# Three kinds of heads: scores and maxima from split q and k for heads 10 to 15, with p and v left whole

## The chip, the cores and the metric

The kernel runs on one core of one Trainium2 chip. A core has a matrix engine (TensorE, PE in the profile), a vector engine (VectorE, DVE), a scalar engine (ScalarE, ACT), a general engine (GpSimd, POOL) and a queue engine that issues transfers (SyncE, SP). Each takes its instructions in the order in which they stand in the program; they wait for one another through semaphores. Matrix products are written to PSUM, of which there are eight banks; everything else on the chip lies in SBUF. The metric is the device time of one execution in microseconds (us), the median of several runs.

## The reference

The first half is causal attention with a decay, over 8 batches of 8 heads, 576 positions and 64 channels (64 heads in all); the second half sends its output through two matrix products with a squared ReLU between them.

```
scores = q @ k.T / 8                     # per head, 576 x 576
cum    = cumsum(log(clip(f, 1e-4, 1)))
scores = where(causal, -1e9, scores + cum[:, None] - cum[None, :])
attn   = exp(scores - max(scores))
attn   = attn / (sum(attn) + 1e-9)
x      = (attn @ v), heads side by side  # 4608 x 512
out    = relu(x @ w_in)**2 @ w_out       # 512 -> 2048 -> 512
```

All is float32. A product of two float32 operands can be computed whole (one matmul on float32 data, which the trace records as two), or split: each operand is written as a rounded high part and a low remainder in the type float32r, and the result is the sum of a few float32r matmuls on these parts.

## The kernel before

**Slots.** The program is a list of slots, written out by a Python loop (L742 to L766). A slot is one *unit* of one head: a block of 128 keys against all the queries that may see it (for the first block, queries 256 to 575, and 0 to 255 as the sixth unit). Six units make a head, 64 heads make 384 slots. In a slot stand, in this order: the scores of the unit (`score`), the product of exponentials and v for the unit of two slots ago (`av_part`), a divide by the row sums that is due (`finish`), and then, in two halves, the events that are listed for this slot, some steps of the weight conversion (`cv`) and some of the second half of the network (`fill`). PE, ACT, DVE and POOL keep to this order; SP's transfers are put in order by the scheduler.

**Scores.** `score` puts scores transposed into a PSUM bank (keys on partitions, queries along the row). Decay and maximum ride along as rows of the operands beyond the 64 channels: k carries the cumulative sum, q carries the negative row maximum. ACT then takes the exponential straight into `p`. Units on the diagonal are masked.

**Two kinds of heads.** Heads 0 to 15 (`NWHOLE = 16`) are *whole*: q and k are loaded as float32 into `rl` (`load_whole`, SP), one float32 matmul makes the scores (L392), a small bf16 matmul adds the mask (L395), p stays float32, and one float32 matmul makes p times v (L456). Heads 16 to 63 are *split*: q and k are loaded once to `qkraw` (`load`, SP), and `prep` makes the parts: two casts on DVE into `rk` (L313, L314), two casts on ACT into `rl` (L315, L318), two subtractions on POOL into `rl` (L321, L324). Two float32r matmuls make the scores (L399, L402), POOL masks p (L411), p and v are split too (`split_p`: L424 on ACT, L425 on DVE; `split_v`: L332 on DVE, L333 on POOL), and p times v takes three float32r matmuls (L435 to L437).

**Maxima.** The row maxima of a head are found one head ahead by six float32r matmuls from `rk` (L346), each of which DVE reduces (L354). For a whole head `rk` is loaded by POOL with a cast during the transfer (`load_rounded`, L287), the six stand in slots 0 to 2.5 of the head before, and the maxima, which come out as a column, are turned into a row by five small matmuls (`turn_maxima`, L377) and two ACT copies (L381). For a split head `rk` comes from the casts, the six stand in slots 1.5 to 4, and each finished column is written to the row of `rk` by a transfer on SP (L359). The casts stand in slot 0.5, POOL's subtractions in slots 1.5 and 3.5.

**Banks.** `bank(use)` hands out PSUM banks in turn. From the first step of the second half on, maxima have no banks of their own and take turns with the scores: four banks at first, two (`s=[1, 2]`) from the first step of the second chunk of 256 tokens on, four again from the third.

**Second half.** `mlp1` (L555, twelve matmuls of 256 columns), ACT and DVE (L563 to L566), `mlp2` (L578, six of 512 columns). 18 chunks times 16 steps; `fill` spreads them over the slots from slot 53 on. Until about slot 95 a step can stand only where its weights are converted: the weights come as 64-bit patterns, and `weight_ops` makes float32 of them and splits it, for each of 32 tiles with ACT (L205, L210), four DVE instructions (L228, L233, L236, L240) and one POOL subtraction (L216).

The head whose scores are computed moves from 9 to 16 between about 97 and 224 us of the profiled execution. In this stage heads 9 to 15 compute scores while weights are still being converted and steps of the second half are already standing between them.

## Time and profile before

| | |
|---|---|
| three runs | 1218.88, 1219.85, 1225.44 us, median 1219.85 us |
| profiled execution | 1217.56 us, of which the span from the first to the last instruction is 1215.8 us |
| busy over the span | PE 1189.4 us (98%), DVE 769.5 (63%), ACT 706.2 (58%), POOL 361.8 (30%) |
| TensorE clock granted | 0.994 of full speed on average |
| PE in 0 to 95 us (start, heads 0 to 8) | busy 84.5 of 95 us |
| PE in 113.59 to 206.30 us (heads 10 to 14) | busy 89.8 of 92.7 us |
| PE in 410 to 800 us (split heads) | busy 389.2 of 390 us |

"Busy" is the time in which at least one instruction of the engine was running. Matmuls overlap in the records (one starts before the last one's results are out), so what a matmul costs in a full stream is not its own duration but the distance from its start to the start of the next one.

### The profile page before, as it was taken

To read this page: it belongs to the slowest core of one execution; us is meant where nothing else is said; L and a number is where in the kernel's file an instruction comes from. 1 tells how busy PE (TensorE), PEld (TensorE's weight loads), DVE (VectorE), ACT (ScalarE), POOL (GpSimd) and SP (SyncE) were. 2 spreads that over 40 slices of the span, in tenths; PEclk is the share of its full clock that TensorE was granted. 3 is DMA by queue.
4 is the path that set the end of the run, shared out by engine and by line. 5 is a ranking of instruction groups with operands and counts; after the bars stand their busy time and mean duration, and the time that the engine had idled before them with its cause. 6 is when DMAs were issued, how large, how long until landed. Compare 5 with 4: busy or idle time off the path is not lost.

```text
span 1215.8 us, 23255 instructions
## 1 busy us (share of the span) xinstructions
PE 1189.4 (98%) x7816; PEld 1047.3 (86%) x7816; DVE 769.5 (63%) x2031; ACT 706.2 (58%) x1736; POOL 361.8 (30%) x551
## 2 busy tenths in 40 slices
PE   6999999899999999999999999999999999999998
PEld 3668787779999898999999989988999899999997
DVE  5767776766767667665655766667676767533332
ACT  3875556566666666655556566666666666533232
POOL 3332322333334333322322333333333333200000
PEclk8999999999999999999999999999999999999999
DMA  7889310111211112111121212212121212000000
GB/s 217 206 198 272 90 42 26 47 46 42 59 42 53 38 47 50 41 49 27 43 55 21 53 32 44 57 42 58 37 50 33 58 43 58 12 28 11 9 18 18
DMA packets 104767, 72.16 MB, mean 59 GB/s; under 512 B 86573, under 2 KB 86573, under 8 KB 104649
## 3 DMA queue, kind: packets, MB, share of 16 engines
q1 hardware_dynamic: 103368, 65.96, 21.2%
q0 software_dynamic: 1280, 4.72, 1.6%
q8 instruction: 62, 1.02, 0.4%
q14 instruction: 57, 0.46, 0.1%
HBM read 60.51 MB, written 9.87 MB: 58 GB/s over the span
## 4 chain that ended last, share of the span: by engine, by line
PE 90%; ACT 4%; DVE 2%; issue 2%; DMA 1%; POOL 0%; SPq 0%; DVEq 0%; POOLq 0%; ACTq 0%
PE bank L555 33%; PE bank L578 31%; PE bank L346 4%; PE bank L392 3%; PE bank L435 3%; PE bank L456 3%; PE bank L402 3%; PE bank L437 3%; PE bank L436 3%; PE bank L399 3%; ACT r L563 1%; DVE bank L354 1%; ACT gh L565 0%; ACT den L471 0%; ACT p L409 0%
## 5 line engine op out<-in xcount | busy, mean ns | idle before, releaser
L578 PE MATMUL bank<-w,gh 128*128 128x512 f32 x1152 | 414.1, 400 | 0.0
L555 PE MATMUL bank<-xh,w 128*128 128x256 f32 x2304 | 329.0, 285 | 1.9 <-POOL w L216 1.9
L555 PEld LDWEIGHTS bank<-xh,w 128*128 128x128 f32 x2304 | 300.3, 189 | 10.3 <-POOL w L216 2.4
L425 DVE TENSOR_TENSOR pl<-p,ph 128x320 fp32r<-128x320 f32 (+4 forms) x288 | 177.4, 616 | 192.8 <-ACT ph L424 188.3
L578 PEld LDWEIGHTS bank<-w,gh 128*128 128x128 f32 x1152 | 217.5, 189 | 38.4
L563 ACT ACTIVATE r<-bank 128x256 f32<-128x256 f32 x288 | 110.6, 384 | 218.4 <-PE bank L555 172.3
L578 PE MATMUL bank<-w,gl 128*128 128x512 f32 x576 | 226.9, 394 | 0.2 <-DVE gl L566 0.2
L564 DVE TENSOR_TENSOR g<-r 128x256 f32<-128x256 f32 x288 | 125.7, 437 | 146.6 <-ACT r L563 146.0
L424 ACT CAST ph<-p 128x320 fp32r<-128x320 f32 (+4 forms) x288 | 119.4, 415 | 145.6 <-POOL p L411 103.0
L411 POOL TENSOR_SCALAR_AFFINE_SELECT p<-p 128x128 f32<-128x128 f32 (+1 forms) x240 | 77.1, 321 | 412.0 <-ACT p L409 317.6
L555 PE MATMUL bank<-xl,w 128*128 128x256 f32 x1152 | 184.5, 282 | 0.0
L555 PEld LDWEIGHTS bank<-xl,w 128*128 128x128 f32 x1152 | 158.2, 191 | 0.2 <-DVE xl L543 0.2
L566 DVE TENSOR_TENSOR gl<-g,gh 128x256 fp32r<-128x256 f32 x288 | 130.3, 452 | 36.2 <-ACT p L409 2.0
L354 DVE CUSTOM_DVE_ANT_0 bank<-bank,mz 128x256 f32<-128x256 f32 (+4 forms) x320 | 133.4, 433 | 22.6 <-PE bank L346 20.5
L409 ACT ACTIVATE p<-bank 128x320 f32<-128x320 f32 (+4 forms) x288 | 111.6, 388 | 60.1 <-PE bank L402 48.9
L565 ACT ACTIVATE gh<-r 128x256 fp32r<-128x256 f32 x288 | 120.6, 419 | 9.4
L346 PE MATMUL bank<-rk 66*128 66x320 f32 (+4 forms) x384 | 110.6, 317 | 13.9 <-DVE tcol L354 11.0
L578 PEld LDWEIGHTS bank<-w,gl 128*128 128x128 f32 x576 | 109.3, 190 | 14.4 <-DVE gl L566 0.9
L435 PE MATMUL bank<-pl,vh 128*65 128x320 f32 (+4 forms) x336 | 93.3, 278 | 2.6 <-ACT den L471 2.6
L346 PEld LDWEIGHTS bank<-rk 66*128 66x128 f32 (+1 forms) x384 | 67.2, 181 | 29.3 <-DVE tcol L354 13.0
L436 PE MATMUL bank<-ph,v 128*64 128x320 f32 (+4 forms) x336 | 91.2, 271 | 0.0
L437 PE MATMUL bank<-ph,vh 128*65 128x320 f32 (+4 forms) x336 | 89.3, 272 | 0.0
(92 smaller groups left out, 1539.0 us busy)
## 6 DMA issues: line engine op xcount, KB each, us to landing
qkraw<-in_qk SPq DMA_DIRECT2D x48, 288.0 KB
v<-in_v SPq DMA_DIRECT2D x64, 160.0 KB
out<-osb SPq DMA_DIRECT2D x36, 256.0 KB
den<-rdr SPq DMA_DIRECT2D x62, 144.0 KB
w<-in_w_in SPq DMA_DIRECT2D x16, 512.0 KB
w<-in_w_out SPq DMA_DIRECT2D x16, 512.0 KB
rl<-in_qk SPq DMA_DIRECT2D x16, 288.0 KB
rk<-in_qk POOLq DMA_DIRECT2D x16, 288.0 KB, 4.4
```

Of the source, the lines that this page charges most:

```text
L346: nc.tensor.matmul(ps[:m, :n], st["r2"][:D + 2, q0:q0 + m], st["kl0"][:D + 2, k0:k0 + n], start=True, stop=True,)
L354: nc.vector.tensor_tensor_reduce(out=ps[:m, :n], in0=ps[:m, :n], in1=mz[:m, mo:mo + n], op0=ALU.add, op1=ALU.min, scale=-1.0, scalar=init, ...
L425: nc.vector.tensor_tensor(out=pl[:kn, :n], in0=p[:kn, :n], in1=ph[:kn, :n].bitcast(F32), op=ALU.subtract,)
L435: nc.tensor.matmul(acc[:D + 1, o], vh, pl[:kn, i], start=first, stop=False)
L436: nc.tensor.matmul(acc[:D, o], vl, ph[:kn, i], start=False, stop=False)
L437: nc.tensor.matmul(acc[:D + 1, o], vh, ph[:kn, i], start=False, stop=last)
L555: nc.tensor.matmul(ph[:, :T], w[:, s, cc], x[:, cc, :], start=(cc == 0 and k == 0), stop=(cc == NCC - 1 and k == 2),)
L563: nc.scalar.activation(out=r, in_=ph[:, :T], func=AF.Relu)
L564: nc.vector.tensor_tensor(out=g, in0=r, in1=r, op=ALU.mult)
L565: nc.scalar.activation(out=gh, in_=r, func=AF.Square)
L566: nc.vector.tensor_tensor(out=gl, in0=g, in1=gh.bitcast(F32), op=ALU.subtract)
L578: nc.tensor.matmul(po, g[:, ts], w[:, s], start=(fc == 0 and k == 0), stop=(fc == NF - 1 and k == 2),)
```

## The change

A second constant is introduced. `NWHOLE` becomes 10 and goes on to decide how scores and maxima are made; the new `NPLAIN = 16` decides how p and v are kept and where the mask is added. So heads 0 to 9 are whole as before, heads 16 to 63 are split as before, and heads 10 to 15 are of a third kind: `load`, `prep`, the maxima and their transfers, and the two float32r score matmuls as for a split head; the mask added by the bf16 matmul, now after the second of the two, and p and v whole as for a whole head. In the changed file all lines after L74 stand one or two further down, and lines of `score` up to seven.

```diff
--- before.py
+++ after.py
@@ -71,7 +71,8 @@
 
     MAG_LOW, MAG_HIGH = struct.unpack("<2f", struct.pack("<2I", 0x38000000, 0x47EFFFFF))
 
-    NWHOLE = 16
+    NWHOLE = 10
+    NPLAIN = 16
     DEPTH = 4
     cpool = ctx.enter_context(tc.tile_pool(name="cpool", bufs=1))
     wk = ctx.enter_context(tc.tile_pool(name="wk", bufs=2))
@@ -299,7 +300,7 @@
         if h < NH:
             vr = state[h]["vr"] = wk.tile([P, NJ, D + 2], F32, name="v", bufs=3)
             nc.sync.dma_start(out=vr[:, :, :D], in_=v[h])
-            if h < NWHOLE:
+            if h < NPLAIN:
                 nc.gpsimd.memset(vr[:, :, D:], 1.0)
 
     def prep(h, part):
@@ -324,7 +325,7 @@
             nc.gpsimd.tensor_tensor(out=r1[D:], in0=q, in1=r1[:D].bitcast(F32), op=ALU.subtract)
 
     def split_v(h):
-        if NWHOLE <= h < NH:
+        if NPLAIN <= h < NH:
             st = state[h]
             vr = st["vr"][:, :, :D]
             vh = st["vh"] = vhs[h % 2]
@@ -386,30 +387,31 @@
         k0, kn = KT[j]
         n = q1 - q0
         ps = bank("s")
+        masked = q0 == k0
+        added = masked and h < NPLAIN
         if h < NWHOLE:
-            masked = q0 == k0
             r, k = st["whole"].q[:D + 3], st["whole"].k[:D + 3]
-            nc.tensor.matmul(ps[:kn, :n], k[:, k0:k0 + kn], r[:, q0:q1], start=True, stop=not masked)
-            if masked:
-                m = min(kn, n)
-                nc.tensor.matmul(
-                    ps[:kn, :m], mz[:kn, MW - P:MW - P + kn], eye[:kn, :m], start=False, stop=True,
-                )
+            nc.tensor.matmul(ps[:kn, :n], k[:, k0:k0 + kn], r[:, q0:q1], start=True, stop=not added)
         else:
             nc.tensor.matmul(
                 ps[:kn, :n], st["kl0"][:D + 3, k0:k0 + kn], st["r2"][:D + 3, q0:q1], start=True, stop=False,
             )
             nc.tensor.matmul(
-                ps[:kn, :n], st["l2"][:, k0:k0 + kn], st["r1"][:, q0:q1], start=False, stop=True,
+                ps[:kn, :n], st["l2"][:, k0:k0 + kn], st["r1"][:, q0:q1], start=False, stop=not added,
             )
-        if h < NWHOLE:
+        m = min(kn, n)
+        if added:
+            nc.tensor.matmul(
+                ps[:kn, :m], mz[:kn, MW - P:MW - P + kn], eye[:kn, :m], start=False, stop=True,
+            )
+        if h < NPLAIN:
             p = wk.tile([P, 448], F32, name=("ph", "pl")[u % 2], bufs=3)
         else:
             p = wk.tile([P, 448], F32, name="p")
         nc.scalar.activation(out=p[:kn, :n], in_=ps[:kn, :n], func=AF.Exp, scale=SCALE)
-        if h >= NWHOLE and q0 == k0:
+        if masked and not added:
             nc.gpsimd.affine_select(
-                out=p[:kn, :min(kn, n)], in_=p[:kn, :min(kn, n)], pattern=[[1, min(kn, n)]],
+                out=p[:kn, :m], in_=p[:kn, :m], pattern=[[1, m]],
                 compare_op=ALU.is_ge, fill=0.0, base=0, channel_multiplier=-1,
             )
         st["p"][u] = p
@@ -451,7 +453,7 @@
         kn = KT[j][1]
         base = 0 if low else QA
         o, i = slice(s0 - base, s1 - base), slice(s0 - q0, s1 - q0)
-        if h < NWHOLE:
+        if h < NPLAIN:
             vr = st["vr"][:kn, j, :D + 1]
             nc.tensor.matmul(acc[:D + 1, o], vr, st["p"][u][:kn, i], start=first, stop=last)
         else:
@@ -745,7 +747,7 @@
         if live:
             h, u = slots[n]
             score(h, u)
-            if h >= NWHOLE:
+            if h >= NPLAIN:
                 unsplit.append((h, u))
         for ha, ua in avs.get(n, ()):
             if ua < NU - 1:
```

Three places show how the instructions move. The first is PE in the second slot of head 10. `bank` is a PSUM bank, `rl` and `rk` are the tiles of q and k, `p,mz` the operands of the mask, `pl` and `ph` hold p of a whole head, `xh`, `xl` and `w` are input and weights of the second half. Before:

```order
L555 MATMUL bank_1397<-xh_1113,w_972 128x256 x8
L555 MATMUL bank_1397<-xl_1114,w_972 128x256 x4
L392 MATMUL bank_1418<-rl 128x320
L395 LDWEIGHTS mz
L395 MATMUL bank_1418<-p,mz 128x128
L456 MATMUL bank_1423<-pl,v 65x256
L456 MATMUL bank_1423<-ph,v 65x128
L346 MATMUL bank_1431<-rk_80 128x448
```

and now:

```order
L557 MATMUL bank_1396<-xh_1111,w_970 128x256 x8
L557 MATMUL bank_1396<-xl_1112,w_970 128x256 x4
L396 MATMUL bank_1417<-rk_79 128x320
L399 MATMUL bank_1417<-rl 128x320
L404 LDWEIGHTS mz
L404 MATMUL bank_1417<-p,mz 128x128
L458 MATMUL bank_1423<-pl,v 65x256
L458 MATMUL bank_1423<-ph,v 65x128
L347 MATMUL bank_1438<-rk_80 128x256
```

One float32 score matmul (one row here, two in the trace) became two float32r ones. The maxima of the next head (`rk_80`) begin only here: the matmul of 256 columns is the first of their six, where before the third of them stood, of 448 columns.

The second place is POOL while heads 11 to 13 are computed. L216 (now L217) makes the low part of a weight tile, L492 (now L494) is the divide of a pair of heads. Before:

```order
L216 TENSOR_TENSOR w_1640<-osb,w_1640 128x512
L303 MEMSET v 128x5x2
L287 DMA rk_79<-in_qk 64x1152
L216 TENSOR_TENSOR w_1727<-osb,w_1727 128x512
L216 TENSOR_TENSOR w_1797<-osb,w_1797 128x512
L303 MEMSET v 128x5x2
L216 TENSOR_TENSOR w_1900<-osb,w_1900 128x512
L287 DMA rk_80<-in_qk 64x1152
```

and now:

```order
L313 MEMSET rl 128x2
L322 TENSOR_TENSOR rl<-qkraw,rk_79 64x576
L217 TENSOR_TENSOR w_1646<-osb,w_1646 128x512
L304 MEMSET v 128x5x2
L325 TENSOR_TENSOR rl<-qkraw,rl 64x576
L217 TENSOR_TENSOR w_1747<-osb,w_1747 128x512
L217 TENSOR_TENSOR w_1814<-osb,w_1814 128x512
L313 MEMSET rl 128x2
L322 TENSOR_TENSOR rl<-qkraw,rk_80 64x576
```

The loads that POOL issued are gone, and for each head two subtractions over 64 x 576 elements stand among the weight subtractions.

The third place is SP while head 9 is computed, where the maxima of head 10 (`rk_79`) and many weight loads are due. Before:

```order
L194 DMA w_1839<-in_w_out 128x1024
L194 DMA w_1931<-in_w_in 128x1024
L194 DMA w_2014<-in_w_out 128x1024
L294 DMA rl<-in_qk 64x1152
L281 DMA rl<-cum_dr 2x576
L194 DMA w_2093<-in_w_in 128x1024
```

and now:

```order
L195 DMA w_1618<-in_w_in 128x1024
L360 DMA rk_79<-tcol 1x128x1
L273 DMA qkraw<-in_qk 64x1152
L360 DMA rk_79<-tcol 1x128x1
L195 DMA w_1692<-in_w_out 128x1024
L360 DMA rk_79<-tcol 1x128x1 x2
L195 DMA w_1775<-in_w_in 128x1024
L360 DMA rk_79<-tcol 1x64x1
```

The five transfers that bring the maxima to their row stand between weight loads, each waiting for DVE's reduction, and the load of the next head's q and k stands between the first and the second of them.

## The prediction

> **What bounds the kernel now.** I read first the busy row and the chain of waits on the page, then the busy time of each engine head by head, then the order of time on PE, DVE and POOL.

> ```profile
> PE 1189.4 (98%) x7816; PEld 1047.3 (86%) x7816; DVE 769.5 (63%) x2031; ACT 706.2 (58%) x1736; POOL 361.8 (30%) x551
> ...
> by line: PE bank L555 32.7%; PE bank L578 31.3%; PE bank L346 4.0%; PE bank L392 3.4%; PE bank L435 3.3%; PE bank L456 3.1%; PE bank L402 2.9%; PE bank L437 2.8%; PE bank L436 2.8%; PE bank L399 2.7%; issue 2.0%; ACT r L563 0.7%; DVE bank L
> ```

> PE is busy for 98% of the span and the chain that ended last consists of its matmuls, so a matmul that goes away shortens the program, as long as the engines that feed PE keep up. That has to be asked of the stage that changes. These windows are cut at the first score of each head, from head 10 (first row) to head 15 (last row):

> ```profile
> core 0: us, PE busy (x) PEld busy (x) DVE busy (x) ACT busy (x) POOL busy (x), PEclk, DMA share, GB/s
> 113.59:131.83 18.24, 18.24 (x117) 15.20 (x115) 14.00 (x34) 11.09 (x26) 3.68 (x5) 1.00 0.74 223
> 131.83:150.44 18.61, 17.26 (x104) 13.67 (x103) 13.08 (x30) 10.10 (x26) 5.82 (x7) 1.00 0.18 44
> 150.44:169.26 18.82, 18.58 (x115) 15.13 (x114) 13.29 (x32) 10.55 (x25) 5.60 (x6) 1.00 0.22 57
> 169.26:186.54 17.28, 17.21 (x109) 14.01 (x108) 12.76 (x31) 10.30 (x24) 4.86 (x5) 1.00 0.12 29
> 186.54:206.30 19.76, 18.49 (x116) 15.22 (x115) 13.47 (x33) 10.24 (x25) 4.01 (x4) 1.00 0.13 37
> 206.30:224.44 18.14, 17.02 (x100) 13.32 (x99) 13.66 (x32) 10.06 (x24) 6.46 (x6) 1.00 0.09 18
> ```

> Heads 10 to 14 take 92.71 us, 18.54 each; PE is busy for 89.78 of them (17.96 a head) and idle for 2.93. DVE is busy for 66.60 (13.32 a head, 72%), ACT for 10.4 a head, POOL for 4.8. So PE sets the pace here too, but DVE is not far behind, and it runs in order.

> **The change, part by part.** *Scores.* The first row below is the score of a 320-column unit of head 15, from its start to the start of the product behind it; the last three are the same unit of the first split head.

> ```profile
> 206.30 0.70 PE L392 MATMUL bank<-rl 67*128 67x320 f32 x2
> 206.84 0.70 PE L456 MATMUL bank<-ph,v 128*65 128x320 f32 x2
> ...
> 224.44 0.31 PE L399 MATMUL bank<-rk 67*128 67x320 f32 x1
> 224.59 0.31 PE L402 MATMUL bank<-rl 128*128 128x320 f32 x1
> 224.73 0.70 PE L456 MATMUL bank<-ph,v 128*65 128x320 f32 x2
> ```

> Whole it holds PE for 206.84 - 206.30 = 0.54 us, split for 224.73 - 224.44 = 0.29 us. A head's six units have 320 + 320 + 192 + 64 + 448 + 256 = 1600 columns, five times as many: 2.70 us against 1.45. The chain gives nearly the same: 3.4% of 1215.8 us over 16 heads is 2.58 us, 2.9% + 2.7% over 48 heads 1.42. I take 1.2 us a head, 7.2 us for six. The mask matmul (L395) and the float32 product with v (L456) stay, at the same cost.

> *Maxima turned into a row.* For heads 10 to 15 the five matmuls of L377 go (they stood in heads 9 to 14).

> ```profile
> 126.43 0.57 PE L377 MATMUL bank<-p 128*65 128x128 f32 x5
> 126.83 1.19 PE L555 MATMUL bank<-xh,w 128*128 128x256 f32 x8
> ...
> 146.19 0.85 PE L377 MATMUL bank<-p 128*65 128x128 f32 x5
> 146.88 1.19 PE L555 MATMUL bank<-xh,w 128*128 128x256 f32 x8
> ```

> Start to start they take 0.40 us in one head and 0.69 in another; the mean, 0.55, times six is 3.3 us. PE loses 7.2 + 3.3 = 10.5 us of work in all. The matmuls of the maxima (L346) stay as many and as long, only one and a half slots later.

> *What the other engines get.* ACT loses two copies a head (L381) and gets two casts; DVE gets two casts, POOL two subtractions:

> ```profile
> L381 ACT COPY rl<-bank 1x512 f32<-1x512 f32 (+1 forms) x32 | 10.9, 388 | 4.9 <-PE bank L377 4.5
> L315 ACT CAST rl<-qkraw 64x576 fp32r<-64x576 f32 x48 | 32.1, 670 | 0.7
> L318 ACT CAST rl<-qkraw 64x576 fp32r<-64x576 f32 x48 | 32.0, 667 | 0.0
> L313 DVE CAST rk<-qkraw 64x576 fp32r<-64x576 f32 x48 | 27.6, 575 | 0.0
> L314 DVE CAST rk<-qkraw 64x576 fp32r<-64x576 f32 x48 | 30.1, 628 | 0.0
> L321 POOL TENSOR_TENSOR rl<-qkraw,rk 64x576 fp32r<-64x576 f32 x48 | 69.9, 1456 | 2.2 <-DVE rk L314 2.2
> L324 POOL TENSOR_TENSOR rl<-qkraw,rl 64x576 fp32r<-64x576 f32 x48 | 68.8, 1433 | 4.0
> ```

> ACT: -2 x 0.39 + 0.67 + 0.67 = +0.56 us, 11.0 of the 16.2 us that PE will need per head (17.96 - 10.5/6): hidden, cost nothing. POOL: +2.9 us, 7.7 of 16.2; hidden as time, but not without effect on DVE. DVE: +1.2 us for the casts. What POOL does to DVE shows in head 15, which already prepares a split head (16) while weights are being converted:

> ```profile
> 210.13 1.80 POOL L321 TENSOR_TENSOR rl<-qkraw,rk 64x576 fp32r<-64x576 f32 x1 [2.22 <-DVE rk L314]
> ...
> 210.57 1.64 DVE L228 TENSOR_SCALAR wmag<-wmag 128x512 f32<-128x512 f32 x1
> ...
> 218.79 0.42 DVE L228 TENSOR_SCALAR wmag<-wmag 128x512 f32<-128x512 f32 x1
> ```

> While L321 ran, from 210.13 to 211.93, an instruction of DVE that takes 0.42 us alone took 1.64. I count 1.2 us of this for L321 and, between 0 and as much, 0.9 for L324. DVE then has 13.3 + 1.2 + 2.1 = 16.6 us of work a head where PE has 16.2. On this the prediction turns: PE will no longer be clearly the slower.

> [...]

> *What PE waits for.* These are the waits of heads 12, 14 and 15, and two behind them:

> ```profile
> 139.95 0.35 PE L346 MATMUL bank<-rk 66*128 66x192 f32 x1 [1.28 <-DVE p L354]
> ...
> 201.22 0.24 PE L377 MATMUL bank<-p 128*65 128x64 f32 x1 [1.27 <-ACT ph L409]
> ...
> 213.57 0.41 PE L346 MATMUL bank<-rk 66*128 66x320 f32 x1 [0.90 <-DVE tcol L354]
> ...
> 218.09 0.36 PE L346 MATMUL bank<-rk 66*128 66x192 f32 x1 [0.23 <-ACT pl L409]
> ...
> 227.32 1.21 PE L555 MATMUL bank<-xh,w 128*128 128x256 f32 x8 [1.89 <-POOL w L216]
> ...
> 252.32 0.41 PE L346 MATMUL bank<-rk 66*128 66x320 f32 x1 [2.16 <-DVE tcol L354]
> ```

> The matmuls of the maxima take turns with the scores on the same banks, so each waits until DVE has reduced the maximum before it or ACT has read the scores before it. Behind a waiting L346 on PE stand the next step of the second half and the next scores, so the wait delays everything. Head 15 is the nearest precedent for heads 10 to 14 after the change: same casts and subtractions, same unsplit p, same two banks. It has 0.90 + 0.23 = 1.13 us of waits, against 2.93/5 = 0.59 in the heads before it. Five heads at 1.13 are 5.65 us, 2.7 more than now. But head 15 converted fewer weights than its neighbours:

> ```profile
> 186.54:206.30 19.76, 2.06 (x3) 1.00 0.13 37
> 206.30:224.44 18.14, 1.92 (x2) 1.00 0.09 18
> ```

> These are the runs of L240, one per weight: two in head 15, three in head 14. A weight costs DVE four instructions of 0.42 (L228) to 0.69 us (2.06/3, L240), some 2.2 us by my estimate, which heads 10 to 14 will have on top. The wait per head is therefore between 1.13 and DVE's whole excess over PE plus that; I take 0.3 us more a head, 1.5 us in all. The wait at 227.32 stays: POOL's program there, around `split_v` of head 16, is the same.

> *Transfers.* The maxima of heads 10 and 11 must now travel by SP's queue between the weight loads, before the head's first score. Between 95 and 131 us the same kind of load took longer to land than later, 8.2 us against 3.7:

> ```profile
> rk<-in_qk POOLq DMA_DIRECT2D x2, 288.0 KB, 8.2
> ...
> rk<-in_qk POOLq DMA_DIRECT2D x2, 288.0 KB, 3.7
> ```

> The first is from the window 95 to 131 us, the second from 131 to 200. If a row of maxima were late by all of the difference, head 10 would start 4.5 us late; if the two slots (some 5.5 us) that the program leaves suffice, not at all. The first unit needs only the maxima of queries 256 to 575, which are issued first, so I take 0.8 us, nearer to nothing. Weight loads that stand behind these transfers on SP come later, but they run several tiles ahead of their use.

> *Sum.* -7.2 - 3.3 + 2.7 + 1.5 + 0.8 = -5.5 us. Against the profiled execution, 1217.56 us, that is 1212.1; the median of the runs shown, 1219.85, lies 2.3 us above it, so the median of the changed kernel should be near 1214 us.

> **The rivals.** *No new waits.* The reductions of the maxima read PSUM, and in head 15 only an instruction on the weights was stretched, so the waits could stay at 0.59 us a head or go altogether with the L377 wait: -10.5 to -13.4 us, 1206 to 1209 on the median. Against it stands DVE's 16.6 us.

> [...]

> *Slower.* Casts of DVE can be caught by POOL's weight subtractions too. Were both casts stretched by 1.2 us like L228 and the subtractions cost DVE twice 1.2, a head would give DVE 13.3 + 1.2 + 2.4 + 2.4 = 19.3 us, more than the 18.54 that it takes now: six heads are 4.6 us late, and a late head 10 adds up to 4.5. That is 1224 to 1229. It decides as soon as DVE's work and unavoidable waits exceed 18.54 us a head. In head 15 DVE had 13.66 us, which speaks against it.

> *Nothing happens at this place*, because PE's records overstate what it is bound by. Start to start distances in full streams make this unlikely.

> **How the numbers follow.** A change of less than 0.5% (6.1 us) cannot be told from none here. The forecast (-3 to -9 us) gets 0.50, no new waits 0.15, DVE takes over 0.20, slower 0.12, nothing 0.03. About half of the forecast's band lies beyond -6.1, a little under, and all of the first rival: 0.24 + 0.15 is about 0.40 for faster. Of the slower rival nearly all is beyond +6.1 only if head 10 starts late too, so with some room for what I do not see I put 0.13. Same is the rest, 0.47. The range for 8 in 10 runs from the first rival's upper half to the lower edge of the slower one: 1207 to 1222 us; the forecast's own is 1211 to 1217.

> **What would show it.** Right: the heads between about 113 and 222 us take some 17.2 us each instead of 18.5, PE busy some 16.2 of them; two float32r matmuls per unit with 0.29 us from start to start at 320 columns; no L377 behind head 9's; DVE busy near 16 us a head with single instructions of 1.2 to 1.8 us beside POOL's subtractions; PE waiting for DVE's reductions some 1.4 us a head. Wrong: PE idle for 2 us or more a head in this stage (DVE takes over), a wait of several us of PE's first score of head 10 or 11 for the transfers of the maxima, a granted clock below 1.00 in this stage, or longer waits for POOL's weight parts than the one at 227 us.

## The result, and the profile after

The changed kernel takes 1225.96 us (median of 12 runs, 1223.18 to 1237.18), the kernel before, in runs taken beside it, 1219.86 us (12 runs, 1217.54 to 1225.44). The ratio is 1.0055, with a 95% interval of 1.0036 to 1.0075: slower by about 6 us, where 5.5 us less was forecast. In the ratios further down, but not in the medians, five executions of 1282 to 4053 us are left out as slow.

The profiled execution of the changed kernel is one of its longer ones: 1229.65 us, with a span of 1227.9 us, 12.1 us more than the profiled execution before. What follows explains these 12.1 us; their split is that of one execution. The first score of head 9 comes at 97.03 us instead of 96.74, that of head 16 at 235.27 instead of 224.44. So 0.3 us come ahead of the stage, 10.5 us within it (138.24 instead of 127.70 us) and 1.3 us behind it.

The busy row of the page hardly moved, except that the loss shows in PE's share:

```profile
PE 1185.9 (97%) x7786; PEld 1045.9 (85%) x7786; DVE 791.7 (64%) x2043; ACT 708.9 (58%) x1736; POOL 380.8 (31%) x563
```

The busy time of each engine head by head, heads 9 to 15, cut at the first score of each head, with the columns that the prediction shows (stretch, length, busy time of PE, PEld, DVE, ACT and POOL, granted clock, share and rate of the DMA):

```profile
97.03:116.44 19.41, 17.09 (x105) 13.62 (x104) 17.94 (x34) 11.76 (x27) 7.35 (x7) 1.00 0.36 101
116.44:133.30 16.86, 16.86 (x109) 14.57 (x110) 14.80 (x36) 11.15 (x26) 6.06 (x6) 1.00 0.73 223
133.30:156.36 23.06, 18.35 (x100) 14.78 (x98) 18.09 (x33) 10.91 (x26) 8.10 (x8) 0.85 0.19 54
156.36:175.56 19.20, 18.22 (x111) 14.32 (x110) 16.66 (x36) 11.18 (x25) 7.50 (x7) 1.00 0.18 42
175.56:193.43 17.87, 15.95 (x105) 13.06 (x104) 16.29 (x32) 10.27 (x24) 9.07 (x9) 1.00 0.13 28
193.43:212.20 18.77, 17.04 (x111) 14.34 (x110) 13.92 (x36) 11.17 (x26) 6.20 (x5) 1.00 0.18 41
212.20:235.27 23.07, 17.95 (x99) 14.46 (x98) 16.22 (x32) 9.98 (x24) 7.70 (x6) 0.85 0.07 15
sum 138.24, PE 121.46 PEld 99.17 DVE 113.92 ACT 76.41 POOL 51.98; mean PE 17.35 PEld 14.17 DVE 16.27 ACT 10.92 POOL 7.43
```

The same stretch of the kernel before, as one window:

```profile
96.74:224.44 127.70, 123.64 (x760) 100.55 (x759) 93.78 (x224) 73.08 (x175) 34.99 (x34) 1.00 0.32 93
```

PE was idle for 127.70 - 123.64 = 4.1 us of this stage before and for 138.24 - 121.46 = 16.8 us after. Heads 11 and 15 are the worst, 23 us each, and in both the granted clock is 0.85 on average. Head 10, within which nothing waits, shows the change as it was meant: 16.86 us instead of 18.24.

What PE waited for in this stage, grouped, from the view of waits (us in total, times, longest):

```profile
PE bank L347 <- DVE tcol L355: 13.5, 7, 4.5
PE bank L394 <- DVE tcol L355: 1.7, 1, 1.7
...
PE bank L396 <- DMA rk<-tcol: 0.4, 1, 0.4
```

Nearly all is one thing: a maximum's matmul (L347) that needs a bank whose maximum DVE has not reduced (L355) yet. The longest of them, in head 11, on POOL, DVE and PE in the order of time:

```profile
136.82 1.45 POOL L494 TENSOR_TENSOR xt<-xt,den 128x576 f32<-128x576 f32 x1 [2.62 <-DMA den<-rdr]
...
138.28 1.57 POOL L322 TENSOR_TENSOR rl<-qkraw,rk 64x576 fp32r<-64x576 f32 x1
139.81 1.45 POOL L217 TENSOR_TENSOR w<-osb,w 128x512 fp32r<-128x512 f32 x1
...
141.39 1.42 POOL L325 TENSOR_TENSOR rl<-qkraw,rl 64x576 fp32r<-64x576 f32 x1
```

```profile
136.91 1.69 DVE L229 TENSOR_SCALAR wmag<-wmag 128x512 f32<-128x512 f32 x1
138.70 1.44 DVE L234 TENSOR_SCALAR osb<-wmag 128x512 int32<-128x512 int32 x1
140.06 1.49 DVE L566 TENSOR_TENSOR g<-r 128x256 f32<-128x256 f32 x1
141.68 1.40 DVE L568 TENSOR_TENSOR gl<-g,gh 128x256 fp32r<-128x256 f32 x1
143.01 0.42 DVE L355 CUSTOM_DVE_ANT_0 bank<-bank,mz 128x256 f32<-128x256 f32 x1
```

```profile
137.97 0.28 PE L347 MATMUL bank<-rk 66*128 66x256 f32 x1
...
143.54 0.64 PE L347 MATMUL bank<-rk 66*128 66x320 f32 x1 [4.47 <-DVE tcol L355]
143.97 0.63 PE L580 MATMUL bank<-w,gh 128*128 128x512 f32 x1
```

For 6 us POOL runs four instructions back to back: the divide of a pair of heads (L494), the change's first subtraction (L322), a weight subtraction (L217), the change's second subtraction (L325). In that time DVE completes four instructions, one per POOL instruction, each of which takes 0.42 to 0.43 us when POOL is quiet: some 4.3 us lost. The first reduction stands behind them in DVE's queue. PE has done everything it may and waits 4.47 us. Then its matmuls (L580) run at 0.63 us where they took 0.40, because the granted clock has fallen to 0.50, already during the wait:

```profile
138.00:141.80 3.80, 1.07 (x8) 0.50 (x6) 3.56 (x4) 2.25 (x6) 3.72 (x6) 1.00 0.20 44
141.80:148.60 6.80, 5.06 (x16) 4.44 (x17) 4.08 (x9) 0.00 (x0) 1.00 (x1) 0.50 0.18 43
148.60:152.00 3.40, 3.15 (x20) 2.37 (x19) 2.14 (x5) 1.42 (x4) 1.07 (x1) 1.00 0.02 0
```

(Same columns as the windows above.) Head 15 has the same picture with three of POOL's instructions (217.50 to 222.38 us), beside which DVE completes two, and a wait of 4.44 us at 223.12.

### The profile page after: what moved, and what is told of

The parts are those of the page before. It is cut to its first block, busy times and chain, and to the rows that moved or that the text cites. A ratio compares the mean times of both kernels' runs of the same rounds, so it can differ in the third digit from the quotient of the medians.

```text
span 1227.9 us, 23291 instructions
## 1 busy us (share of the span) xinstructions
PE 1185.9 (97%) x7786; PEld 1045.9 (85%) x7786; DVE 791.7 (64%) x2043; ACT 708.9 (58%) x1736; POOL 380.8 (31%) x563
## 4 chain that ended last, share of the span: by engine, by line
PE 82%; DVE 7%; ACT 3%; issue 3%; DMA 3%; POOL 1%; SPq 0%; DVEq 0%; POOLq 0%; ACTq 0%
PE bank L557 30%; PE bank L580 29%; PE bank L347 4%; PE bank L437 3%; PE bank L399 3%; PE bank L396 3%; PE bank L439 3%; PE bank L438 3%; PE bank L458 2%; PE bank L394 2%; DVE bank L355 1%; DVE g L566 1%; DVE osb L237 1%; ACT r L565 1%; DVE osb L234 1%
## 5 line engine op out<-in xcount | busy, mean ns | idle before, releaser
L580 PE MATMUL bank<-w,gh 128*128 128x512 f32 x1152 | 415.5, 401 | 0.0
L557 PEld LDWEIGHTS bank<-xh,w 128*128 128x128 f32 x2304 | 302.2, 190 | 10.4 <-POOL w L217 2.6
L580 PEld LDWEIGHTS bank<-w,gh 128*128 128x128 f32 x1152 | 218.5, 190 | 38.6
L580 PE MATMUL bank<-w,gl 128*128 128x512 f32 x576 | 227.8, 395 | 0.1
L566 DVE TENSOR_TENSOR g<-r 128x256 f32<-128x256 f32 x288 | 132.0, 458 | 135.2 <-ACT r L565 134.9
L568 DVE TENSOR_TENSOR gl<-g,gh 128x256 fp32r<-128x256 f32 x288 | 134.2, 466 | 35.4 <-PE bank L580 0.5
L355 DVE CUSTOM_DVE_ANT_0 bank<-bank,mz 128x256 f32<-128x256 f32 (+4 forms) x320 | 133.2, 433 | 23.7 <-PE bank L347 22.1
L347 PE MATMUL bank<-rk 66*128 66x320 f32 (+4 forms) x384 | 111.5, 319 | 28.8 <-DVE tcol L355 24.1
L580 PEld LDWEIGHTS bank<-w,gl 128*128 128x128 f32 x576 | 109.7, 191 | 14.5 <-DVE gl L568 0.9
L347 PEld LDWEIGHTS bank<-rk 66*128 66x128 f32 (+1 forms) x384 | 67.7, 182 | 47.4 <-DVE tcol L355 30.0
L437 PE MATMUL bank<-pl,vh 128*65 128x320 f32 (+4 forms) x336 | 93.2, 277 | 2.3 <-ACT den L473 2.3
L399 PE MATMUL bank<-rl 128*128 128x320 f32 x324 | 95.1, 294 | 0.0
L396 PE MATMUL bank<-rk 67*128 67x320 f32 x324 | 93.5, 289 | 0.5 <-DMA rk<-tcol 0.4
## 6 DMA issues: line engine op xcount, KB each, us to landing
qkraw<-in_qk SPq DMA_DIRECT2D x54, 288.0 KB
rl<-in_qk SPq DMA_DIRECT2D x10, 288.0 KB
```

What stands on the lines that cost most here:

```text
L347: nc.tensor.matmul(ps[:m, :n], st["r2"][:D + 2, q0:q0 + m], st["kl0"][:D + 2, k0:k0 + n], start=True, stop=True,)
L355: nc.vector.tensor_tensor_reduce(out=ps[:m, :n], in0=ps[:m, :n], in1=mz[:m, mo:mo + n], op0=ALU.add, op1=ALU.min, scale=-1.0, scalar=init, ...
L396: nc.tensor.matmul(ps[:kn, :n], st["kl0"][:D + 3, k0:k0 + kn], st["r2"][:D + 3, q0:q1], start=True, stop=False,)
L399: nc.tensor.matmul(ps[:kn, :n], st["l2"][:, k0:k0 + kn], st["r1"][:, q0:q1], start=False, stop=not added,)
L437: nc.tensor.matmul(acc[:D + 1, o], vh, pl[:kn, i], start=first, stop=False)
L557: nc.tensor.matmul(ph[:, :T], w[:, s, cc], x[:, cc, :], start=(cc == 0 and k == 0), stop=(cc == NCC - 1 and k == 2),)
```

## The experiments

**The theories.** *A*: POOL's instructions stretch DVE's, and those that stand in a run just ahead of the first maximum make PE wait; *A2* is its later form, in which the change's subtractions are two of four in that run. *B*: DVE's own load decides (two casts a head more, all else as much as before). *C*: the transfers of the maxima on SP (in the trace above PE waits 0.44 us for them, once). *D*: two banks for scores and maxima are too few. *Q* and *T* are named where they come up. In some expectations the head with the first long wait is called 12, for the head whose maxima are made there; it is head 11 by its scores. "Stage" is the time from the first score of head 9 to that of head 16 in the profiled execution. Each ratio is to runs of the kernel before taken beside that kernel (their medians lie between 1218.85 and 1221.60 us), so rows are best compared by ratios.

| kernel | median us | ratio to before | stage us | PE idle in it |
|---|---|---|---|---|
| before | 1219.86 | | 127.70 | 4.1 |
| changed | 1225.96 | 1.0055 (1.0036 to 1.0075) | 138.24 | 16.8 |
| subtractions left out | 1223.52 | 1.0034 (1.0018 to 1.0050) | 130.62 | 10.6 |
| before, with added subtractions | 1222.67 | 1.0029 (1.0012 to 1.0046) | 130.03 | 5.5 |
| subtractions in later slots | 1230.90 | 1.0091 (1.0061 to 1.0121) | 139.18 | 17.1 |
| divide later | 1224.48 | 1.0033 (1.0014 to 1.0052) | 133.72 | 13.2 |
| subtractions on DVE | 1228.05 | 1.0074 (1.0047 to 1.0100) | 136.00 | 14.4 |
| all on DVE | 1220.63 | 1.0003 (0.9980 to 1.0026) | 126.91 | 9.2 |
| weights later in the head | 1226.72 | 1.0063 (1.0040 to 1.0086) | 133.65 | 13.7 |
| second maximum later | 1227.97 | 1.0075 (1.0046 to 1.0105) | 132.32 | 12.3 |
| divide's transfers on POOL | 1233.24 | 1.0092 (1.0065 to 1.0118) | 139.51 | 15.2 |
| first maximum early | 1222.63 | 1.0011 (0.9992 to 1.0030) | 128.84 | 10.5 |
| the same, divide later | 1221.91 | 1.0014 (0.9997 to 1.0031) | 129.90 | 9.7 |
| first maximum early, all on DVE | 1215.33 | 0.9954 (0.9935 to 0.9972) | 124.70 | 6.0 |
| the same edits without the change | 1218.64 | 0.9987 (0.9969 to 1.0005) | 125.90 | 1.8 |
| early, weights on DVE, divide later | 1220.04 | 1.0002 (0.9985 to 1.0019) | 127.46 | 7.5 |
| the same, subtractions on DVE too | 1214.71 | 0.9950 (0.9931 to 0.9969) | 120.20 | 4.4 |

### POOL's subtractions left out, and added to the kernel before

The subtraction for q is replaced in the same way as that for k, which the first diff shows.

```diff
-            nc.gpsimd.tensor_tensor(out=l2, in0=k, in1=st["kl0"][:D, :S].bitcast(F32), op=ALU.subtract)
+            if h < NPLAIN:
+                nc.gpsimd.memset(f32(l2), 0.0)
+            else:
+                nc.gpsimd.tensor_tensor(out=l2, in0=k, in1=st["kl0"][:D, :S].bitcast(F32), op=ALU.subtract)
```

> The changed kernel, with POOL's two subtractions of each of heads 10 to 15 (rl<-qkraw,rk and rl<-qkraw,rl, 1.45 us each) replaced by a memset of the same tile; the low parts of q and k of these heads are thereby left out of the result, PE's work is the same. Theory A (POOL's subtractions stand back to back with its weight subtractions and the divide of a pair of heads, 136.82 to 142.8 us in the changed kernel, and in that time DVE finishes one instruction per POOL instruction, 1.4 to 1.7 us instead of 0.42, so the first maximum is reduced late, PE waits 4.47 us twice and its clock falls to half): the waits of 4.4 us in heads 12 and 15 shrink below 1.5 us, the granted clock stays at 1.00 there, 1210 to 1217 us against 1226 for the changed kernel, so a ratio of 0.992 to 0.998 to the kernel before. Rival B (DVE's own two added casts a head and the later slots of the maxima are enough): 1222 us or more, ratio 1.002 or more. Rival C (transfers of the maxima on SP): as B.

```diff
+    def scratch(h):
+        x = rounded[h % 2]
+        for a, n in ((0, 5), (5 * D, 4)):
+            q, k = (
+                y[:D, a:a + n * D].bitcast(F32).rearrange("p (n d) -> p n d", d=D) for y in (x.q, x.k)
+            )
+            nc.gpsimd.tensor_tensor(out=vhs[1][:D, :n, :D], in0=q, in1=k, op=ALU.subtract)
...
+        if 10 <= h < 16:
+            at((h - 1) * NU, 1, scratch, h)
+            at((h - 1) * NU + 2, 1, scratch, h)
```

> The kernel before, with four more POOL subtractions per head in heads 9 to 14 (64x320, 64x256, and again two slots later, into a tile that nobody reads then): POOL's added load of the change alone, without its casts, its later maxima or its float32r scores; the output is unchanged. Theory A: DVE's instructions beside them are stretched to 1 us and more, reductions of maxima come late, 3 to 10 us slower than the kernel before, ratio 1.0025 to 1.008. Rivals B and C: POOL has slack (4.8 of 18.5 us a head), so nothing changes, ratio 0.999 to 1.0015.

Without the subtractions 1223.52 us, some 2.4 of the 6 us back: well above what A expected, and in the band of B and C. Head 11's wait fell from 4.47 to 2.35 us and cost one step of clock instead of two. Head 15 still waited 3.09 us, since the subtractions made there are head 16's, which this edit leaves on POOL. With added subtractions in the kernel before 1222.67 us: +3.5 us from work of POOL alone, on an engine that was idle for some 70% of this stage, with no change on DVE or PE. (POOL's busy time in the stage rose by 22.9 us, more than the 17.0 of the change.) That is A's band; B and C expected nothing. So POOL's instructions do cost time, but the two subtractions are only part of it. In the first kernel the rest of the run was still there, and the memsets were no empty place either:

```profile
134.73 1.58 POOL L500 TENSOR_TENSOR xt<-xt,den 128x576 f32<-128x576 f32 x1 [1.87 <-DMA den<-rdr]
...
136.28 0.58 POOL L323 MEMSET rl<- 64x576 f32 x1
136.82 1.44 POOL L217 TENSOR_TENSOR w<-osb,w 128x512 fp32r<-128x512 f32 x1
```

```profile
134.95 2.19 DVE L229 TENSOR_SCALAR wmag<-wmag 128x512 f32<-128x512 f32 x1
137.25 1.34 DVE L234 TENSOR_SCALAR osb<-wmag 128x512 int32<-128x512 int32 x1
```

(L500 is the divide in this kernel, L323 the memset.) One instruction of DVE took 2.19 us, through divide and memset, the next 1.34, through the weight subtraction; in the changed kernel both take 0.42 with POOL quiet.

### The subtractions or the divide later

```diff
-                at((h - 1) * NU + SPLIT[part], 1, prep, h, part)
+                late = h < NPLAIN and part > 1
+                at((h - 1) * NU + (part + 1 if late else SPLIT[part]), int(not late or part == 2), prep, h, part)
```

> The changed kernel, with POOL's two subtractions of heads 10 to 15 two and a half and half a slot later (both of them behind the first four reductions of the maxima instead of the first one ahead of all). Theory A: the first maximum no longer waits behind a run of four POOL instructions; the two 4.4 us waits shrink to about 2, 1213 to 1220 us, ratio 0.995 to 1.000, with some waits of PE for the low parts or the last maxima left. Rival B: DVE has the same work in all, 1224 to 1228 us, ratio 1.003 to 1.007.

```diff
+        if part == 3 and h in (9, 11, 13):
+            return (h + 2) * NU + 5
         return (h + 1) * NU - 1 + DIVIDE[h >= H][part]
```

> The changed kernel, with POOL's divide of heads 8+9, 10+11 and 12+13 (1.45 us each) five slots later, so that it no longer stands just ahead of the subtractions for heads 12, 14 and 16; no work is added or left out. Theory A, in the form that the length of POOL's uninterrupted run decides: the waits of 4.47 and 4.44 us fall by at least 1.4 us each, and the clock loss behind them (some 2.5 us each) goes, 1215 to 1221 us, ratio 0.997 to 1.001. If any subtraction of POOL counts and not the run: 1223 to 1226, ratio 1.003 to 1.006. Rival B: no change from the changed kernel, 1.0055.

The first gave 1230.90 us, slower still, and above B's band too. In heads 9 to 14 the first subtraction began 7.9 to 10.6 us into the head instead of 3.3 to 5.0, and now stood close ahead of the second. In head 11, which begins at 133.88 us in this kernel:

```profile
142.09 1.55 POOL L322 TENSOR_TENSOR rl<-qkraw,rk 64x576 fp32r<-64x576 f32 x1
143.71 1.77 POOL L325 TENSOR_TENSOR rl<-qkraw,rl 64x576 fp32r<-64x576 f32 x1
```

Head 11's wait fell from 4.47 to 2.25 us and its clock stayed at 1.00, as A said. Head 15's wait stayed at 4.43 us: head 16's subtractions, which are made there, were not moved. And new waits came, at later maxima: of scores for reductions (1.29 us in head 12, where the clock fell, and 0.91) and of head 14 for its row of maxima (1.56). A was right about the first maximum and wrong about the whole: the harm moved with the subtractions.

The second moved the divide. Head 15 fell from 23.07 to 17.14 us and its wait from 4.44 to 1.00, head 11 only from 23.06 to 21.37, and head 14 rose from 18.77 to 21.02, because its wait (1.84 instead of 1.73 us) now had a step of clock behind it. The median, 1224.48 us, lies in the band of A's second form: every subtraction of POOL counts, not only the run. Why head 15 had been harmless before is seen in the order of time. These are the first of the divide's transfers on SP, the divide, and what follows on POOL, first in the kernel before, then in the changed one; head 15 begins at 206.30 and at 212.20 us:

```profile
192.91 0.51 SPq L481 DMA_DIRECT2D cmp<-den  x1
...
205.05 1.59 POOL L492 TENSOR_TENSOR xt<-xt,den 128x576 f32<-128x576 f32 x1 [5.57 <-DMA den<-rdr]
206.60 1.27 POOL L216 TENSOR_TENSOR w<-osb,w 128x512 fp32r<-128x512 f32 x1
...
213.71 1.30 POOL L216 TENSOR_TENSOR w<-osb,w 128x512 fp32r<-128x512 f32 x1 [1.77 <-ACT w L210]
```

```profile
199.27 0.53 SPq L483 DMA_DIRECT2D cmp<-den  x1
...
213.27 1.44 POOL L494 TENSOR_TENSOR xt<-xt,den 128x576 f32<-128x576 f32 x1 [8.03 <-DMA den<-rdr]
214.67 1.47 POOL L217 TENSOR_TENSOR w<-osb,w 128x512 fp32r<-128x512 f32 x1
...
217.50 2.12 POOL L322 TENSOR_TENSOR rl<-qkraw,rk 64x576 fp32r<-64x576 f32 x1 [1.33 <-DVE rk L315]
219.58 1.26 POOL L217 TENSOR_TENSOR w<-osb,w 128x512 fp32r<-128x512 f32 x1
220.92 1.46 POOL L325 TENSOR_TENSOR rl<-qkraw,rl 64x576 fp32r<-64x576 f32 x1
```

Before, the divide began 1.25 us ahead of the head, POOL had caught up by the first subtraction, and the next weight subtraction came 1.8 us behind that one (which ran from 210.13 to 211.93). Now it begins 1.07 us into the head: head 14 became 1.0 us shorter (18.77 instead of 19.76), and from the first transfer to the divide, by way of an SP queue that now holds the rows of maxima too, it takes 14.0 us instead of 12.1. Everything behind it on POOL closes up.

### The subtractions, then all of POOL's two-operand work, on DVE

```diff
-            nc.gpsimd.tensor_tensor(out=l2, in0=k, in1=st["kl0"][:D, :S].bitcast(F32), op=ALU.subtract)
+            (nc.vector if h < NPLAIN else nc.gpsimd).tensor_tensor(out=l2, in0=k, in1=st["kl0"][:D, :S].bitcast(F32), op=ALU.subtract)
```

> The changed kernel, with POOL's two subtractions of each of heads 10 to 15 done by DVE (all of the computation is kept). Theory A2 (after the first four runs: every POOL instruction that stands beside DVE stretches a DVE instruction to its own length, and the change's subtractions are two of the four in the run ahead of the first maximum, the others the weight subtraction and the divide that were there before): DVE does 2 x 0.7 us more itself and is stretched by 2 x 1.0 to 1.2 less, so like the kernel without them or better, 1220 to 1224 us, ratio 1.000 to 1.004. Rival B (DVE's own amount of work decides): DVE gets 1.4 us a head more, 1228 or more, ratio 1.007 or more.

```diff
+                engine = nc.vector if late[0] else nc.gpsimd
+                engine.tensor_tensor(out=hl[:, 1], in0=w, in1=hl[:, 0].bitcast(F32), op=ALU.subtract)
...
+            engine = nc.vector if h in (9, 11, 13) else nc.gpsimd
+            engine.tensor_tensor(out=x, in0=x, in1=den, op=ALU.mult)
...
+        late[0] = 9 * NU <= n
```

(On DVE the weight subtraction stands one step of the conversion later.)

> The changed kernel, with all of POOL's two-operand instructions of this stage done by DVE: the two subtractions of heads 10 to 15, the weight subtractions from head 9 on and the divides of pairs 8+9, 10+11 and 12+13. DVE's instructions of 1.2 us and more go, and with them the waits of PE for the first maximum. Theory A2: DVE gains 1.4 + 2.7 x 0.7 = 3.3 us of work of its own a head and loses about five stretches of 1.0 to 1.2; waits below 1.5 us, no loss of clock, 1209 to 1217 us, ratio 0.992 to 0.998. Rival B: DVE at 18 us a head or more, 1230 us or more.

The subtractions alone on DVE: 1228.05 us, within the band of B, not to be told from the changed kernel. The run on POOL still had the divide and the weight subtraction (wait of 3.67 us in head 11), DVE had the first subtraction, 0.74 us, more ahead of the maximum, and head 16's subtractions, which are made in head 15, were still POOL's (4.43 us). With all of it on DVE but head 16's two: 1220.63 us, 0.52% below the changed kernel by the ratios (1.0003 and 1.0055), although DVE now has 23.6 us more of its own in the stage (12 subtractions of 0.74, 18 weight subtractions of 0.69, three divides of 0.75), 3.4 a head. Its busy time even fell, from 113.92 to 105.85 us. B's 1230 us and more are refuted: the 33 instructions had cost DVE 8.1 + 23.6 = 31.7 us while POOL did them, some 0.96 us each, more than the 0.69 to 0.75 that they cost it when it does them itself. A2's 1209 to 1217 us did not come either: 9.2 us of idle time are left, 2.97 of them in head 15 and 1.74 in head 12, where the clock fell.

### Order around the first maximum

```diff
+        if 9 * NU <= n < 15 * NU:
+            wr *= 0 if n % NU < 2 else 1.5
         cv(wr / 2)
```

> The changed kernel, with no weight conversion in the first two slots of heads 9 to 14 and half as much again in the other four: neither DVE's four weight instructions nor POOL's weight subtraction stands ahead of the first maximum of the next head; no work is added or left out. Theory A2: POOL's run loses its middle, DVE has spare time ahead of the first maximum, the two waits of 4.4 us fall to below 2 and the clock stays at 1.00, 1213 to 1220 us, ratio 0.995 to 1.000; the waits later in a head may grow to 1 us each, which is the upper end. Rival D (two banks for scores and maxima are too few, whatever DVE has to do): the waits stay, 1224 us or more, ratio 1.004 or more.

```diff
-        for i, x in enumerate(MAXIMA[split]):
+        for i, x in enumerate((1.5, 2.5, 3, 3.5, 4, 4.5) if 10 <= h < 16 else MAXIMA[split]):
```

> The changed kernel, with the second to the sixth maximum of heads 10 to 15 half a slot later, the first where it is: between the first and the second, which waits for the reduction of the first, PE gets half a slot of work more (some 1.4 to 1.5 us). Theory A2 (the first reduction is late by what POOL does to DVE): the waits of 4.4 us fall to 2.9 to 3.2, still long enough for the clock to fall, those of 1.5 and 1.7 go, 1219 to 1223 us, ratio 1.000 to 1.003. Rival D (the turn of two banks): the waits go nearly all, 1213 to 1218. If the last maxima then reach their row too late, PE waits for that transfer at a head's first score, up to 1.5 us a head, and it is no gain at all.

```diff
-                at((h - 1) * NU + SPLIT[part], 1, prep, h, part)
+                at((h - 1) * NU + SPLIT[part], int(part > 0 or h > 16), prep, h, part)
-        for i, x in enumerate(MAXIMA[split]):
+        for i, x in enumerate((1, 2, 2.5, 3, 3.5, 4) if 10 <= h < 17 else MAXIMA[split]):
```

> The changed kernel, with the casts of heads 10 to 16 half a slot earlier and their first maximum half a slot earlier too (slots 1, 2, 2.5, 3, 3.5, 4 instead of 1.5 to 4): the first reduction then stands on DVE ahead of the second half's two instructions and of the weight instructions of that slot, and the second maximum, which waits for it, comes a whole slot behind it. Theory A2 (all the loss comes from the first reduction standing behind stretched instructions): the waits for the second maximum fall below 1 us, the clock stays at 1.00, 1214 to 1220 us, ratio 0.995 to 1.000. Rival B (the sum of DVE's work per head): the waits move to the later maxima, 1223 us or more.

> The kernel of the run before this one (first maximum and casts early), with the divide of the pairs 8+9, 10+11 and 12+13 five slots later as well, so that POOL's run ahead of the maxima is three instructions at most. Theory A2: no wait over 1.5 us in heads 9 to 15 but that of the first score of head 10 for the rows of maxima, 1211 to 1217 us, ratio 0.993 to 0.998, the 8 us of matrix work that the change saves arriving for the first time. Rival B: 1222 or more.

Weights later in the head: head 11's wait fell from 4.47 to 1.34 us as A2 said, but eight others of 0.5 to 1.3 us stand in the stage, and head 15's, where the edit moves nothing, is still 3.14; 1226.72 us, D's side. Second maximum later: 4.47 became 3.24 us (A2: 2.9 to 3.2, D: gone), yet the median, 1227.97 us, lies above both bands; the clock fell in heads 11 and 14, and head 10 now waited 1.72 us for its row of maxima. Head 15's wait fell from 4.44 to 1.62 us here, although the edit leaves the maxima made there in their places: it hangs on when things fall together. First maximum early: head 15's long wait went, the longest in the stage is 1.85 us, the clock stays at 1.00 in all of it; 1222.63 us, 0.44% below the changed kernel by the ratios, but between what A2 and B gave. With the divide later on top 1221.91, no further gain that can be told, at the edge of B's band. So the place of the first reduction was one part of it; with that mended, 10 us of PE idle time remained, spread over the other maxima.

### The divide's transfers off SP

```diff
+        queue = nc.gpsimd if h in (9, 11, 13) else nc.sync
-                nc.sync.dma_start(out=st["cmp"][i * D:(i + 1) * D], in_=den[i * D:i * D + 1, :])
+                queue.dma_start(out=st["cmp"][i * D:(i + 1) * D], in_=den[i * D:i * D + 1, :])
```

(The other two transfers of `finish` alike.)

> The changed kernel, with the transfers of the divide (cmp<-den, rdr<-cmp, den<-rdr) of pairs 8+9, 10+11 and 12+13 issued by POOL's queue instead of SP's. Theory Q: these transfers now stand on SP between the rows of maxima (rk<-tcol), each of which waits for DVE; den<-rdr goes out 10.5 us behind cmp<-den instead of 8.9 (heads 14 and 13's pair), the divide starts 1.1 us behind the first score of head 15 instead of 1.3 us ahead of it, and so POOL's divide, weight subtraction and the two subtractions stand back to back ahead of the first maximum. Off SP the divide starts 1.5 us or more earlier relative to the head, the waits of 4.4 us in heads 11 and 15 fall to below 2.5 us, 1217 to 1222 us, ratio 0.998 to 1.002. If the length of POOL's own work decides and not when the divide comes: 1224 to 1227, and POOL waiting for its own transfers may make it worse.

1233.24 us, by its ratio as slow as the later subtractions, and no test of Q: POOL issues in order as well, stood 2.9 us for DVE ahead of one of the transfers of each pair, and the divide of head 11 began 4.9 us into the head instead of 3.5. How much of its lateness comes from SP's queue and how much from shorter heads stays open.

### Early and all on DVE, with and without the change

> First maximum and casts early, and POOL's divides, weight subtractions from head 9 on and the two subtractions of heads 10 to 16 done by DVE. Theory A2: as the run before, or better by what the remaining stretches cost, 1210 to 1217 us; should DVE's own work, then 17 us or more a head, become the limit, 1217 to 1222. Rival B: 1225 or more.

This is the first kernel faster than the one before: 1215.33 us, ratio 0.9954. The edits are those of "first maximum early" and "all on DVE", head 16 included. The next three kernels ask what of that is the change's.

> The kernel before, with all that the run with 1215 us had beside the change (weight subtractions from head 9 on, the divides of three pairs and head 16's subtractions on DVE, head 16's casts and first maximum half a slot earlier), and without the change itself. Theory A2 (the matrix work saved arrives in full once POOL no longer stretches DVE): the difference between this kernel and that one is the 7 to 9 us of matrix work, so this one is at 1219 to 1224 us, ratio 0.999 to 1.003. Rival T (the 1215 us come from taking work off POOL, which the kernel before gains from just as much): 1213 to 1217, ratio 0.994 to 0.998.

> The changed kernel with casts and first maximum early, the divides five slots later on POOL, the weight subtractions from head 9 on done by DVE; POOL keeps the change's two subtractions a head, alone and not in a run. Theory A2, single stretches of 1.0 to 1.2 us fall beside waiting time: 1212 to 1217 us, ratio 0.993 to 0.998. If each stretch counts, in a run or alone: two a head, 1217 to 1221.

> As the run before, and the two subtractions of heads 10 to 16 on DVE too, so that POOL has only the three divides, five slots late. Against the kernel with 1215 us DVE no longer waits for the divide's transfer (1.9 us idle ahead of the divide in head 11, PE 1.69 us). Theory A2: 1211 to 1215 us, ratio 0.992 to 0.996. If DVE's own work (some 15 us a head) is what is left: 1215 to 1218.

The same edits without the change give 1218.64 us, not to be told from the kernel before. T had given a ratio of 0.994 to 0.998, of which the interval (0.9969 to 1.0005) reaches only the upper part: the kernel before has 0.31% to gain from a quiet POOL at most, the changed one got 1.0% by the same edits (1.0055 to 0.9954). The last two kernels differ in nothing but who makes the change's subtractions (head 16's too), and by 5.3 us: 1220.04 us with POOL, 1214.71 with DVE. With POOL they stand alone, but for heads 11 and 13, where the second runs into the late divide; and they still cost 0.5%. In head 14 a lone one, at 192.17 us, stretched a weight instruction of DVE (L244) from 0.69 to 1.44 us, and the wait behind it is 1.82 us with a step of clock, where it is 1.23 us without one when DVE does them. A2's "run" was too narrow, single ones count too. The last kernel beats the changed one and the kernel before, the latter by 0.5% (0.31% to 0.69%).

Set beside the kernel with the early edits and no change, it also weighs the change's matrix work, since the clock stays up in both. (They differ in one thing more: the three divides are DVE's in the first, POOL's and later in the second.) Heads 9, 10 and 15 and the sum of seven, first without the change, then with it:

```profile
97.54:114.38 16.84, 16.84 (x110) 13.97 (x109) 13.36 (x34) 10.77 (x26) 0.75 (x2) 1.00 0.81 252
114.38:132.61 18.23, 18.23 (x117) 15.19 (x115) 13.66 (x37) 10.96 (x26) 0.83 (x2) 1.00 0.76 214
...
206.26:223.44 17.18, 16.95 (x100) 13.20 (x98) 13.97 (x37) 10.10 (x24) 0.00 (x0) 1.00 0.09 19
sum 125.90, PE 124.07 PEld 100.42 DVE 92.89 ACT 73.00 POOL 3.04; mean PE 17.72 PEld 14.35 DVE 13.27 ACT 10.43 POOL 0.43
```

```profile
98.53:115.34 16.81, 16.63 (x105) 13.57 (x104) 15.37 (x38) 11.52 (x26) 0.40 (x2) 1.00 0.48 145
115.34:132.12 16.78, 16.78 (x111) 14.50 (x110) 15.43 (x41) 11.41 (x26) 0.28 (x2) 1.00 0.70 221
...
202.21:218.73 16.52, 16.02 (x100) 12.85 (x98) 13.13 (x36) 10.07 (x24) 0.00 (x0) 1.00 0.09 18
sum 120.20, PE 115.77 PEld 95.48 DVE 104.47 ACT 76.48 POOL 5.20; mean PE 16.54 PEld 13.64 DVE 14.93 ACT 10.93 POOL 0.74
```

PE's busy time falls by 124.07 - 115.77 = 8.3 us. Of that 2.6 us come back as waits (4.43 us idle instead of 1.83). The stage is 5.7 us shorter; 1.0 us is lost again because head 9 starts later in this execution and 0.9 behind the stage, so the two spans differ by 3.8 us, and the medians by 3.9 (A2 had expected 7 to 9 between the kernels with and without the change).

## Why the prediction was wrong

**Matrix work: right.** Forecast -10.5 us. Counted as the forecast counts, from the start of a matmul to the start of the next and without waits, the scores of heads 9 to 15 take 19.0 us in the kernel without the change (2.71 a head) and 12.1 in the last kernel (some 1.57 a head for heads 10 to 15), and 3.5 us of turned maxima (L377) go: 10.4 us. PE's busy time fell by 8.3 only, because some of it came back at matmuls that the change leaves alone: from start to start the products with v take 15.4 us instead of 13.4, the masks 2.3 instead of 1.9. Head 9 shows the difference: its five matmuls for turned maxima held PE for 0.40 us, and without them it is busy for 0.21 us less (16.84 - 16.63). The likely reason, not shown, is that PE waits more often there, and a matmul ahead of a wait counts with its whole duration.

**What the other engines get.** The totals held: DVE 16.27 us a head (forecast 16.6), ACT 10.9 (11.0), POOL 7.4 (7.7). Head 10 waited 0.44 us for its row of maxima (0.8; between nothing and 1.84 in the kernels run).

**Waits: the step that failed.** The prediction took the waits of heads 10 to 14 from head 15 of the kernel before (1.13 us, "the nearest precedent"), with 0.3 us for the weights on top: +4.2 us in all, and 0.8 for the rows of maxima. PE's idle time rose by 16.8 - 4.1 = 12.7 us. By the windows, heads 10 to 14 were idle for 9.34 us instead of 2.93 (+6.4), head 15 for 5.12 instead of 1.12 (+4.0), and head 9 for 2.32 instead of nothing. The last two had been put at nothing. Head 9 now makes the maxima of a split head as heads 10 to 14 do; 1.72 us of its waits are for a reduction and 0.44 for the row of maxima. Head 15 itself, whose order on DVE and POOL did not change, went from 0.90 to 4.44 us of wait for its second maximum. So a wait of this kind is no property of a head's work: it depends on how POOL's instructions fall in time, and in the precedent the divide came 2.3 us earlier in the head. The prediction counted one stretched instruction per subtraction, as a load to be averaged over a head, and did not ask what POOL's own queue looks like when four such instructions meet just ahead of the reduction that PE needs next. (It also put the wait at 139.95 us in head 12; it is in head 11.)

**A term that was missing.** The clock fell during both long waits, for 6.83 us each time. Of these 1.75 and 2.82 us lay within the wait; for the other 5.1 and 4.0 us PE worked at half the clock, which cost some 4.5 us (half of the 9.1, an estimate). The stage adds up to its 10.5 us: from start to start scores and turned maxima took 10.1 us less than in the kernel before, PE was idle for 12.7 us more, and the other matmuls took 7.9 us more. The clock is 4.5 of the 7.9; the rest stands mostly at the products with v (2.8 us) and stays open as above. The prediction named a clock below 1.00 as a sign of being wrong, and gave it no price. All this is one execution. Over its 12 runs the changed kernel had a mean granted clock of 0.989, the kernel before, beside the experiments, 0.991 to 0.992; by span times lost clock that is an estimate of 3 to 4.4 us, so a good part of the 6 us is clock in the other runs too.

**The rivals.** The time fell into the band of "slower" (1224 to 1229 us, chance 0.12), in the right place, but not by its condition: it was to decide when DVE's work and unavoidable waits exceed 18.54 us a head. DVE had 16.27 of work; which of its waits were unavoidable no run shows. Nor were it mainly the casts that were caught: 4 of 14 were, at 0.99 us, the others took 0.45. "DVE takes over" (1216 to 1220 us, chance 0.20), in which DVE's work and the waits it cannot avoid set the pace of a head, treated DVE as a rate, and missed for the same reason. That DVE's load could lie above the forecast's 16.6 us a head was the author's assumption, and the run does not show it: 16.27. The kernel with 1214.71 us shows that the forecast of 1214 was reachable by further edits, with DVE at 14.9 us a head and POOL nearly silent (0.7).

**What is stretched.** POOL does not stretch all of DVE's instructions alike. This is L355, the reduction, which reads a bank and one tile, and L566, which reads two tiles, over the stage (the duration columns are ns, least, median and most):

```profile
L355 DVE CUSTOM_DVE_ANT_0 bank<-bank,mz x35: 217/420/633, 105.9 to 232.1; 128x256 f32<-128x256 f32 x7, 128x448 f32<-128x448 f32 x7, 128x320 f32<-128x320 f32 x7, 128x192 f32<-128x192 f32 x7
L566 DVE TENSOR_TENSOR g<-r x27: 407/425/2839, 97.6 to 234.1; 128x256 f32<-128x256 f32 x27
```

Sorted by whether POOL was running a two-operand instruction beside them, the reductions of 320 columns take 0.53 us beside and 0.52 alone, those of 448 columns 0.62 and 0.63; L566 takes 1.17 us beside (9 of 27) and 0.42 alone. Why the one and not the other is not shown: L234, which reads one tile, was stretched too (1.44 us at 138.70, 0.42 alone). For what POOL does to DVE the prediction had counted 2.1 us a head: DVE's busy time rose from 13.40 to 16.27 us a head, of which 1.1 are the casts and 1.8 the rest. What the prediction did not work out is the queue: the reduction is not stretched, it only stands behind what is.

**What stays open.** Why only 3.9 of the 8.3 us reach the median even with POOL silent is shown for one execution (2.6 us of waits for DVE, mostly the last maximum made in head 12 at 1.74 us and the fourth in head 14 at 1.23, the rest outside the stage), not settled for the median; the mean granted clock was 0.990 with the change and 0.9915 without, by the same estimate 1.4 us of it. Nor is the share of SP's queue in the late divide settled.

## What to carry to other kernels

A two-operand instruction on POOL is not free because POOL is idle: here it held up one DVE instruction (not a reduction) for about as long as it ran (in head 11 four of 1.40 to 1.69 us beside four of 1.42 to 1.57), so a 1.45 us subtraction on POOL cost DVE about 1 us (0.96 as the mean of 33 instructions), more than the 0.74 us of doing it there. Where PE waits for DVE's results one by one, look at what stands in DVE's queue ahead of that result and what POOL runs at that moment, not at busy time per head. And a precedent for a wait holds only if the neighbours on the other queues fall at the same time; work taken off the pacing engine shifts what waits for a transfer later in the head, here the divide from 1.25 us ahead of head 15 to 1.07 us into it.
